# Attention scores as one fp32 product per block instead of three fp32r products, in a kernel of attention, expert layer and FFN

## The chip, the cores and the metric

The kernel runs on one core of a Trainium2 chip. The metric is device time in microseconds (us) of the whole program. A measurement of this kernel is the median of several executions; the profile is one further execution with the hardware profiler on.

## The reference, cut to what matters

Three stages follow each other: block-causal attention (4 batches, 8 heads, 576 rows, head size 64), an expert layer in which each token goes to one of 8 experts, and a dense feed-forward layer (FFN). The change touches only the first stage, and in it only how the scores are made.

```python
# q, k, v: (4, 8, 576, 64)
scores = scale * np.matmul(q, k.transpose(0, 1, 3, 2))      # scale = 1/8
mask = block_i >= block_j                                   # blocks of 64 rows
scores = np.where(mask, scores, -1000000000.0)
scores = scores - np.max(scores, axis=-1, keepdims=True)
attn = np.exp(scores)
attn = attn / (np.sum(attn, axis=-1, keepdims=True) + 1e-09)
attn_out = np.matmul(attn, v)
x = _moe_ref(attn_out as (2304, 512), w_gate, w1, w2)       # argmax expert, two products
return _moe2_ref(x, w_in, w_out)                            # softplus FFN
```

## The kernel before

**Order of the work.** Every engine runs its instructions in the order in which the program issues them, and that order is written out by hand: `SCHEDULE` is a list of step names, and the program calls the steps one after the other. A step belongs to one or two engines, and waits are placed where a tile is written and read. So the order on each engine is the order of its steps in the list.

**Attention.** Two heads of a batch make a pair; there are 16 pairs, and the steps of a pair carry its number (`S1.10` is a step of pair 10). The first head lies in partitions 0 to 63 and the second in 64 to 127 of the transposed operands, so the score products of the two heads (`j` = 0 and 1) use the upper and the lower half of the rows of TensorE's array. The 576 query rows are cut into five chunks: chunk 0 of 64 rows and chunks 1 to 4 of 128 rows; the masks leave 64, 192, 320, 448 and 576 key columns (`NK`) for them. The steps of a pair, in about their order:

- `Kta`, `Qta` (`prep_pe`, L317): four TensorE transposes each of a pair's k and q rows 0 to 511 into a PSUM tile `psT`. `Ktb`, `Qtb`: one transpose each of the last 64 rows.
- `Kha`, `Qha`, `Khb`, `Qhb` (`prep_hi`, L336): ScalarE (ACT) writes the rounded high part of the transposed operand as fp32r, q times 1/8. `Kla`, `Qla`, `Klb`, `Qlb` (`prep_lo`, L342): VectorE (DVE) subtracts that from the original and writes the low part. `kZ` and `qZ` hold both parts.
- `S0`, `S1`, `S2` (`scores`, L348): the score products. `S0` makes chunk 4 of head 0 (576 columns, as two products of 288) and chunks 3 and 0 of head 1 (448 and 64 columns); `S1` makes chunks 3 and 0 of head 0 and chunk 4 of head 1; `S2` makes chunks 2 and 1 of both (320 and 192 columns). Each product is made three times: high by high, low by high, high by low. A short bf16 product of 64 columns adds the mask to the last block of each chunk but chunk 0.
- `m` (`s_max`): the row maximum on DVE, for one chunk and head. `e` (`s_exp`): exponential and row sum on ACT. `T` (`t_pe`): TensorE transposes of the exponentials, 30 a pair, into `pt`. `h` (`t_out`): copies of `pt` into `PT`, banks 0 and 1 on ACT, banks 2 and 3 on DVE.
- `V` (`pv`): twelve fp32 products of `PT` with v; the two heads use the left and the right 64 columns of the array. `F`, `Xa`, `Xb` (`x_pe`): five fp32 products of 144 columns that transpose the result back and make gate logits; `xa`, `xb` (`x_out`): DVE reads them out of PSUM and divides by the row sums.

A pair's products and maxima run one pair ahead of its `T` and `V`, and its transposes of q and k one pair ahead of that. So between `S0` of a pair and the next pair's `S0` TensorE does, in this order: `T`s with the next pair's `Kta` and `Qta` between them, `Xa` and `Xb`, more `T`s, `Ktb` and `Qtb`, `S1`, `S2`, seven `T`s, `V`.

**PSUM.** The pool `pss` has three tiles for `psT` and for the score tiles `s`; `ps1` has two for `pt`; `ps2` has one, which chunk 4's scores (`s4`) and the five products of `x_pe` (`psx`) take in turn; `pso` has one for `V`.

**Loads.** The raw tiles of k, q and v have five column groups; the fifth holds the last 64 rows, which is half a tile, and is loaded twice, into both halves of the partitions.

In the later pairs steps of the expert routing (`er...`) and the first weight conversions of the expert layer stand between the steps of attention, on DVE, ACT and TensorE.

Of the kernel before, what the change touches and what calls it, by code (L numbers as in the profile page):

```python
# [46 lines left out]
f4 f5 at f6 f7 p0 f0 f1 p1 f2 p2 f3 p3 p4 p5 f8 f9 f10 f11 f12 f13 p6 f14 f15 p7 f16 f17 f18 p8 f19 f20 f21 p9 f22 f23  # L47
f24 f25 p10 f26 f27 f28 p11 f29 f30 p12 f31 f32 f33 p13 f34 p14 f35 f36 p15 f37 p16 f38 f39 p17 f40 f41 f42 p18 f43
b1.0 b1.1 p19 b1.2 b1.3 p20 b1.4 b1.5 p21 b1.6 b1.7 b1.8 p22 u0 Kta.0 b1.9 b1.10 b1.11 p23 b1.12 b1.13 p24 b1.14 b1.15
b1.16 p25 b1.17 Kha.0 p26 p27 p28 Qta.0 p29 Kla.0 p30 Ktb.0 p31 Qtb.0 p32 Qha.0 p33 p34 Qhb.0 p35 Khb.0 Qla.0 p36 Qlb.0  # L50
Klb.0 u1 S0.0 m40.0 Kta.1 Qta.1 m31.0 Kha.1 Qha.1 m01.0 et Kla.1 e31.0 Qla.1 Ktb.1 Qtb.1 e40.0 S1.0 Qhb.1 e01.0 Qlb.1
# [5 lines left out]
Ktb.3 Qtb.3 h01.1 h21.1 S1.2 b2.0 La.0 b2.1 b2.2 b2.3 Qhb.3 b2.4 b2.5 Khb.3 b2.6 b2.7 Qlb.3 b2.8 b2.9 Klb.3 b2.10 b2.11
m30.2 S2.2 m41.2 e30.2 m20.2 T11.1 e41.2 m00.2 T30.1 m10.2 e00.2 m21.2 h11.1 m11.2 e20.2 h30.1 V.1 e10.2 e21.2 e11.2
Xr.2 F1.1 S0.3 F0.1 m40.3 T10.2 T20.2 m31.3 h10.2 Kta.4 e40.3 h20.2 T00.2 Qta.4 m01.3 Kha.4 T31.2 h00.2 Kla.4 Xa.1
Qha.4 h31.2 e31.3 Xb.1 Qla.4 T21.2 e01.3 xa.1 T01.2 xb.1 xo.1 Ktb.4 Qtb.4 h01.2 h21.2 S1.3 La.1 Qhb.4 Khb.4 Qlb.4 Klb.4  # L60
m30.3 S2.3 m41.3 e30.3 m20.3 T11.2 e41.3 m00.3 T30.2 m10.3 e00.3 m21.3 h11.2 m11.3 e20.3 h30.2 V.2 e10.3 e21.3 e11.3
# [5 lines left out]
h21.4 S1.5 La.3 Qhb.6 Khb.6 Qlb.6 Klb.6 m30.5 S2.5 m41.5 e30.5 m20.5 T11.4 e41.5 m00.5 T30.4 m10.5 e00.5 m21.5 h11.4
m11.5 e20.5 h30.4 V.4 e10.5 e21.5 e11.5 Xr.5 F1.4 S0.6 F0.4 m40.6 T10.5 T20.5 m31.6 h10.5 Kta.7 e40.6 h20.5 T00.5 Qta.7
m01.6 Kha.7 T31.5 h00.5 Kla.7 Xa.4 Qha.7 h31.5 e31.6 Xb.4 Qla.7 T21.5 e01.6 xa.4 T01.5 xb.4 xo.4 Ktb.7 Qtb.7 h01.5
h21.5 S1.6 b3.0 La.4 b3.1 b3.2 b3.3 Qhb.7 b3.4 b3.5 Khb.7 b3.6 b3.7 Qlb.7 b3.8 b3.9 Klb.7 b3.10 b3.11 m30.6 S2.6 m41.6  # L70
e30.6 m20.6 T11.5 e41.6 m00.6 T30.5 m10.6 e00.6 m21.6 h11.5 m11.6 e20.6 h30.5 V.5 e10.6 e21.6 e11.6 Xr.6 F1.5 S0.7 F0.5
m40.7 T10.6 T20.6 m31.7 h10.6 Kta.8 e40.7 h20.6 T00.6 Qta.8 m01.7 Kha.8 T31.6 h00.6 Kla.8 Xa.5 Qha.8 h31.6 e31.7 Xb.5
Qla.8 T21.6 e01.7 xa.5 T01.6 xb.5 xo.5 Ktb.8 Qtb.8 h01.6 h21.6 S1.7 La.5 Qhb.8 Khb.8 Qlb.8 Klb.8 m30.7 S2.7 m41.7 e30.7
m20.7 T11.6 e41.7 m00.7 T30.6 m10.7 e00.7 m21.7 h11.6 m11.7 e20.7 h30.6 V.6 e10.7 e21.7 e11.7 Xr.7 F1.6 S0.8 F0.6 m40.8
T10.7 T20.7 m31.8 h10.7 Kta.9 e40.8 h20.7 T00.7 Qta.9 m01.8 Kha.9 T31.7 h00.7 Kla.9 Xa.6 Qha.9 h31.7 e31.8 Xb.6 Qla.9
T21.7 e01.8 xa.6 T01.7 xb.6 xo.6 Ktb.9 Qtb.9 h01.7 h21.7 S1.8 La.6 Qhb.9 Khb.9 Qlb.9 Klb.9 m30.8 S2.8 m41.8 e30.8 m20.8
T11.7 e41.8 m00.8 T30.7 m10.8 e00.8 m21.8 h11.7 m11.8 e20.8 h30.7 V.7 e10.8 e21.8 e11.8 Xr.8 F1.7 S0.9 b3.12 F0.7 b3.13
b3.14 b3.15 b3.16 b3.17 m40.9 T10.8 T20.8 m31.9 h10.8 Kta.10 e40.9 h20.8 T00.8 Qta.10 m01.9 Kha.10 T31.8 h00.8 Kla.10
Xa.7 Qha.10 h31.8 e31.9 Xb.7 Qla.10 T21.8 e01.9 xa.7 T01.8 xb.7 xo.7 Ktb.10 Qtb.10 h01.8 h21.8 S1.9 La.7 Qhb.10 Khb.10
Qlb.10 Klb.10 m30.9 S2.9 m41.9 e30.9 m20.9 T11.8 e41.9 m00.9 T30.8 m10.9 e00.9 m21.9 h11.8 m11.9 e20.9 er0 h30.8 V.8  # L80
e10.9 er1 er2 e21.9 er3 er4 e11.9 er5 er6 er39 Xr.9 F1.8 S0.10 F0.8 m40.10 T10.9 T20.9 m31.10 h10.9 Kta.11 e40.10 h20.9
T00.9 Qta.11 m01.10 Kha.11 T31.9 h00.9 Kla.11 Xa.8 Qha.11 h31.9 e31.10 Xb.8 Qla.11 T21.9 e01.10 xa.8 T01.9 xb.8 xo.8
Ktb.11 Qtb.11 h01.9 h21.9 S1.10 La.8 Qhb.11 Khb.11 Qlb.11 Klb.11 m30.10 S2.10 m41.10 e30.10 m20.10 T11.9 e41.10 m00.10
T30.9 m10.10 e00.10 m21.10 er7 h11.9 er8 m11.10 e20.10 er9 er40 er10 er41 e10.10 er11 er42 er12 h30.9 V.9 e21.10 er13
er14 e11.10 er15 er16 er17 Xr.10 er18 er19 er20 er21 er60 wl0 er22 er23 er24 F1.9 wl4 S0.11 F0.9 wl5 m40.11 T10.10 wl6
T20.10 m31.11 h10.10 Kta.12 e40.11 h20.10 wl3 T00.10 Qta.12 m01.11 Kha.12 T31.10 wl7 h00.10 Kla.12 Xa.9 Qha.12 h31.10
e31.11 Xb.9 Qla.12 T21.10 e01.11 xa.9 T01.10 xb.9 xo.9 Ktb.12 Qtb.12 h01.10 h21.10 S1.11 La.9 Qhb.12 Khb.12 Qlb.12
Klb.12 m30.11 S2.11 m41.11 e30.11 m20.11 T11.10 e41.11 m00.11 T30.10 m10.11 e00.11 m21.11 er25 h11.10 er26 m11.11
e20.11 er27 h30.10 V.10 e10.11 er28 er29 e21.11 er30 er31 er33 er32 e11.11 er34 er44 er35 er67 er36 er68 er37 er38
Xr.11 er43 F1.10 er45 S0.12 er61 er46 er62 er47 F0.10 er48 er49 er50 er51 m40.12 T10.11 T20.11 m31.12 h10.11 Kta.13  # L90
e40.12 h20.11 T00.11 Qta.13 m01.12 Kha.13 er52 er53 T31.11 h00.11 Kla.13 Xa.10 Qha.13 er63 h31.11 e31.12 Xb.10 xa.10
# [1431 lines left out]
```

## Time and profile before

| | |
|---|---|
| median of 3 runs | 924.22 us (923.73, 924.22, 932.33) |
| profiled execution | 922.65 us, of which 920.8 us from the first to the last instruction |
| mean granted TensorE clock | 0.994 |
| TensorE busy (matmul) | 898.9 us, 98% |
| VectorE / ScalarE busy | 665.1 us, 72% / 567.8 us, 62% |
| first and last score product | 7.8 us and 215.6 us after the start |

The busy share of TensorE is that of overlapping intervals with modelled ends: a product's shown duration is longer than the time after which the next one starts. So costs are read from starts: from the start of one group of products to the start of the next. Attention takes somewhat more than the first 229 us of the span, with 16 pairs of nearly the same pattern; the rest is the expert layer and the FFN.

### The profile page before, as it was taken

The page shows a single profiled execution, that of the slowest core. Times are in us where ns is not written, and L with a number is a line of the kernel's source. Part 1 is how long each engine was busy: PE and PEld are TensorE (multiplying, and loading weights), DVE is VectorE, ACT ScalarE, POOL GpSimd, SP SyncE. Part 2 cuts the span into 40 slices and gives each one's busy share as a digit, 9 for nine tenths or more (in the row PEclk, how much of TensorE's full clock was granted, in tenths as well). Part 3 has the DMA queues.
Part 4 walks back from the last instruction along what each step waited for, and adds up shares of the span by engine and source line. Part 5 has one row for each costly group of instructions (what it writes and reads, how often), then busy time and mean ns, then how long its engine had stood idle before and what let it go on. Part 6 is the DMA issues. An engine that isn't in the chain of part 4 may idle for free.

```text
span 920.8 us, 18350 instructions
## 1 busy us (share of the span) xinstructions
PE 898.9 (98%) x6340; PEld 793.8 (86%) x6340; DVE 665.1 (72%) x1476; ACT 567.8 (62%) x1256; POOL 137.5 (15%) x181
## 2 busy tenths in 40 slices
...
GB/s 136 190 173 71 141 84 155 68 51 117 173 52 234 106 303 266 245 224 210 209 42 25 86 236 221 173 177 217 234 294 176 227 302 136 145 120 158 120 79 103
DMA packets 138741, 149.17 MB, mean 162 GB/s; under 512 B 70927, under 2 KB 96015, under 8 KB 138640
## 3 DMA queue, kind: packets, MB, share of 16 engines
...
q10 hardware_dynamic: 1344, 0.33, 0.2%
q14 instruction: 50, 0.41, 0.1%
...
## 4 chain that ended last, share of the span: by engine, by line
PE 57%; DVE 4%; DMA 4%; issue 1%; ACT 1%; SPq 0%; DVEq 0%
PE hps L973 3%; PE hps L974 3%; PE hps L975 3%; PE yps L993 3%; PE yps L995 3%; PE yps L994 3%; PE fh L1138 3%; PE fh L1139 3%; PE fh L1137 3%; PE fX L1138 2%; PE fX L1139 2%; PE fX L1137 2%; PE fY L1138 2%; DMA gq<-gd 2%; PE fY L1139 2%; PE fY L1137 2%
## 5 line engine op out<-in xcount | busy, mean ns | idle before, releaser
L1267 ACT CAST ah<-sum 128x1280 fp32r<-128x1280 f32 (+1 forms) x40 | 46.3, 1157 | 107.5 <-DVE sum L1260 35.7
L973 PE MATMUL hps<-xh,H1h 128*128 128x256 f32 x384 | 109.2, 284 | 1.1 <-DVE hl L983 1.1
L974 PE MATMUL hps<-xl,H1h 128*128 128x256 f32 x384 | 108.9, 284 | 0.3 <-DVE xl L963 0.3
L975 PE MATMUL hps<-xh,H1l 128*128 128x256 f32 x384 | 108.8, 283 | 0.0
L385 ACT ACTIVATE P<-s,negm 128x448 f32<-128x448 f32 (+4 forms) x160 | 82.7, 527 | 25.4 <-DVE negm L380 25.4
L936 DVE TENSOR_TENSOR H2l<-R,H2h 128x512 fp32r<-128x512 f32 x96 | 66.5, 709 | 26.7 <-ACT H2h L932 26.7
L380 DVE TENSOR_REDUCE negm<-s 128x1 f32<-128x576 f32 (+4 forms) x160 | 68.1, 478 | 19.7 <-PE s L374 19.7
L993 PE MATMUL yps<-H2h,hh 128*128 128x512 f32 x192 | 77.4, 403 | 2.1 <-PEq L1463 2.1
L932 ACT CAST H2h<-R 128x512 fp32r<-128x512 f32 x96 | 57.9, 620 | 32.4 <-DVE H2l L936 17.8
L973 PEld LDWEIGHTS hps<-xh,H1h 128*128 128x128 f32 x384 | 73.7, 192 | 1.9 <-DVE hl L983 1.3
L995 PE MATMUL yps<-H2l,hh 128*128 128x512 f32 x192 | 75.0, 391 | 0.0
L994 PE MATMUL yps<-H2h,hl 128*128 128x512 f32 x192 | 74.8, 390 | 0.0
L974 PEld LDWEIGHTS hps<-xl,H1h 128*128 128x128 f32 x384 | 73.7, 192 | 0.9 <-DVE xl L963 0.5
L936 DVE TENSOR_TENSOR H1l<-R,H1h 128x512 fp32r<-128x512 f32 x96 | 64.8, 713 | 13.1 <-ACT H1h L932 12.1
L975 PEld LDWEIGHTS hps<-xh,H1l 128*128 128x128 f32 x384 | 73.7, 192 | 0.0
L391 PE MATMUL pt<-ident,P 128*128 128x128 f32 x480 | 69.4, 282 | 2.7 <-DVE PT L396 2.0
...
L932 ACT CAST H1h<-R 128x512 fp32r<-128x512 f32 x96 | 55.1, 619 | 18.7 <-PE hps L974 17.3
L374 PE MATMUL s<-kZ,qZ 64*128 64x288 f32 (+4 forms) x576 | 62.7, 330 | 2.3 <-DVE kZ L345 1.3
L1271 DVE TENSOR_TENSOR al<-sum,ah 128x1280 fp32r<-128x1280 f32 (+1 forms) x40 | 54.3, 1356 | 14.3 <-ACT ah L1267 14.3
L374 PEld LDWEIGHTS s<-kZ,qZ 64*128 64x128 f32 x576 | 52.9, 195 | 10.4 <-issue 6.3
L391 PEld LDWEIGHTS pt<-ident,P 128*128 128x128 f32 x480 | 53.8, 143 | 6.4 <-DVE PT L396 2.7
(330 smaller groups left out, 2616.5 us busy)
## 6 DMA issues: line engine op xcount, KB each, us to landing
...
```

The lines of the kernel that those rows point to most:

```text
L374: mm(o, lhsT=a, rhs=b, start=first, stop=last)
L380: nc.vector.tensor_reduce(m[0:n], SC[p, j, c][0:n], axis=AX.X, op=ALU.max, negate=True)
L385: nc.scalar.activation(t[0:n, 0:NK[c]], SC.pop((p, j, c))[0:n], AF.Exp, bias=NM.pop((p, j, c))[0:n], scale=1.0, accum_out=rs[p % 4][0:n, c ...
L391: nc.tensor.transpose(ps[:, o:o + 128], P[p, j, c][:, 128 * kc:128 * kc + 128], ident)
L932: nc.scalar.copy(HW[l, i][0], raw(l, i))
L936: TT(l_, raw(l, i), h.bitcast(F32), op=ALU.subtract)
L973: mm(a, lhsT=wh, rhs=xh, start=(k == 0), stop=False)
L974: mm(a, lhsT=wh, rhs=xl, start=False, stop=False)
L975: mm(a, lhsT=wl, rhs=xh, start=False, stop=(k == 3))
L993: mm(o, lhsT=h[:, c], rhs=wh, start=(f == 0), stop=False)
L994: mm(o, lhsT=l[:, c], rhs=wh, start=False, stop=False)
L995: mm(o, lhsT=h[:, c], rhs=wl, start=False, stop=(f == 7))
```

## The change

The scores of a block are one product of unsplit fp32 operands instead of three fp32r products. What follows from it in the code:

- `Z` holds one fp32 copy of each transposed operand. k is copied by ACT (`nc.scalar.copy`), q is multiplied by 1/8 by DVE (`tensor_scalar`), and the low-part steps `Kla`, `Qla`, `Klb`, `Qlb` are gone, as is ACT's work for q.
- The last 64 rows of q are loaded into the lower half of k's fifth column group, and one transpose makes both (`Ktb`; `Qtb` is gone). Of the 44 first loads 38 are left, and 16 instead of 18 for each later batch.
- Chunk 0's product uses its own 64 query rows as weights (64 array columns) and not 128 any more.
- The products of the two heads are issued so that the columns sent to each stay level (`sent`), and no longer by index.
- In `SCHEDULE` the removed steps are taken out, `Qha` and `Qhb` stand at about the places of the old `Qla` and `Qlb`, and some first loads, memsets and later loads move by a few places. All steps after attention keep their order.

```diff
 def prep_pe(p, nm, part):
         b, hp = divmod(p, H // 2)
+        ps = PS[p, nm if part == "a" else "4"] = pss.tile([128, 512], F32, tag="s", name="psT")
+        for i, c in enumerate(range(4) if part == "a" else [4]):
+            t = raw[b, nm][:, c, 2 * hp:2 * hp + 2, :].rearrange("p h d -> p (h d)")
+            nc.tensor.transpose(ps[:, 128 * i:128 * i + 128], t, ident)
+
+    def prep_out(p, nm, part):
         if part == "a":
...
+            Z[p, nm] = work.tile([128, S], F32, tag=nm + "Z", name=nm + "Z", bufs=2)
+            src, o = PS.pop((p, nm)), Z[p, nm][:, 0:512]
         else:
...
-        nc.scalar.activation(Z[p, nm][:, 0, sl], src, AF.Copy, scale=0.125 if nm == "q" else 1.0)
-
-    def prep_lo(p, nm, part):
-        src, sl = prep_src(p, nm, part)
-        z = Z[p, nm]
-        nc.vector.scalar_tensor_tensor(z[:, 1, sl], src, 0.125 if nm == "q" else 1.0, z[:, 0, sl].bitcast(F32), op0=ALU.mult, op1=ALU.subtract)
+            x = {"k": 0, "q": 64}[nm]
+            src, o = PS[p, "4"][:, x:x + 64], Z[p, nm][:, 512:576]
+        if nm == "k":
+            nc.scalar.copy(o, src)
+        else:
+            nc.vector.tensor_scalar(o, src, 0.125, None, op0=ALU.mult)
...
             for c, off in what:
-                o, w = SPAN[c][0], NK[c]
+                (o, n), w = SPAN[c], NK[c]
                 out = SC[p, j, c] = s[:, off:off + w]
                 for a, m in ([(0, w)] if w <= 512 else [(0, 288), (288, 288)]):
-                    end = a + m == w
-                    for x, y in ((0, 0), (1, 0), (0, 1)):
-                        last = (x, y) == (0, 1) and not (c and end)
-                        l.append((out[:, a:a + m], q_[x][:, o:o + 128], k_[y][:, a:a + m], (x, y) == (0, 0), last))
+                    l.append((out[0:n, a:a + m], q_[:, o:o + n], k_[:, a:a + m], True, not c or a + m < w))
                 if c:
                     l.append((out[:, w - 64:w], mrow[64 * j:64 * j + 64], mcol[64 * j:64 * j + 64], False, True))
             lists.append(l)
-        for i in range(max(map(len, lists))):
-            for l in lists:
-                if i < len(l):
-                    o, a, b, first, last = l[i]
-                    mm(o, lhsT=a, rhs=b, start=first, stop=last)
+        sent = [0, 0]
+        while any(lists):
+            j = min((i for i in range(2) if lists[i]), key=lambda i: sent[i])
+            o, a, b, first, last = lists[j].pop(0)
+            sent[j] += o.shape[1]
+            mm(o, lhsT=a, rhs=b, start=first, stop=last)
```

Of the schedule, these lines show the pattern of the first pairs:

```diff
-T20.0 m31.1 h10.0 Kta.2 e40.1 h20.0 T00.0 Qta.2 m01.1 Kha.2 Xr.0 T31.0 h00.0 Kla.2 Qha.2 T21.0 h31.0 e31.1 Ktb.2 Qla.2
+e21.0 m40.1 T10.0 e11.0 T20.0 m31.1 h10.0 Kta.2 e40.1 h20.0 T00.0 Qta.2 m01.1 Kha.2 Xr.0 T31.0 h00.0 T21.0 h31.0 e31.1
```

On TensorE, at `S0` of a middle pair, the program before has this order. `s_1197` is the tile of chunk 4 of head 0, the other `s` that of chunks 3 and 0 of head 1, `mcol,mrow` is the mask; the last row is the first `T`. A product of 128 output rows uses 128 columns of the array.

```order
L374 MATMUL s_1197<-kZ,qZ 128x288
L374 LDWEIGHTS mrow
L374 MATMUL s<-mcol,mrow 128x64
L374 MATMUL s_1197<-kZ,qZ 128x288
L374 MATMUL s<-kZ,qZ 128x64
L374 MATMUL s_1197<-kZ,qZ 128x288
L374 MATMUL s<-kZ,qZ 128x64
L374 LDWEIGHTS mrow
L374 MATMUL s_1197<-mcol,mrow 128x64
L374 MATMUL s<-kZ,qZ 128x64
L391 MATMUL pt<-ident,P_0_124 128x128 [waits PE_49]
```

The changed program has this order at the same place (its `scores` is at L357, its `T` at L374).

```order
L357 MATMUL s_1206<-kZ,qZ 128x288 [waits PE_49]
L357 MATMUL s<-kZ,qZ 128x448 [waits PE_49,Activation_49]
L357 MATMUL s_1206<-kZ,qZ 128x288
L357 LDWEIGHTS mrow
L357 MATMUL s<-mcol,mrow 128x64
L357 MATMUL s<-kZ,qZ 64x64
L357 LDWEIGHTS mrow
L357 MATMUL s_1206<-mcol,mrow 128x64
L374 MATMUL pt<-ident,P_2_134 128x128 [waits PE_49]
```

Six products and three short ones of chunk 0 have become two and one, and chunk 0's product, of 64 output rows now, stands between two mask products of 128 output rows.

On DVE, between the row maxima of `S0` and those of `S1`, the program before has this order (`kZ`, `qZ` at L345 are the low parts, `PT` at L396 the copies `h`, `xs` and `lg` the steps `xa` and `xb`).

```order
L380 TENSOR_REDUCE negm<-s 64x1
L345 SCALAR_TENSOR_TENSOR kZ<-psT,kZ 128x512 [waits Activation_49]
L396 COPY PT_1463<-pt 128x320 [waits PE_49]
L345 SCALAR_TENSOR_TENSOR qZ<-psT,qZ 128x512 [waits Activation_49]
L439 TENSOR_TENSOR xs<-psx,rinv 128x384 [waits DMAHW7_49,DMAHW6_49,PE_49]
L440 TENSOR_TENSOR lg<-psx,rinv 128x48 [waits Pool_49]
L439 TENSOR_TENSOR xs<-psx,rinv 128x256
L440 TENSOR_TENSOR lg<-psx,rinv 128x32
L396 COPY PT_1492<-pt 128x512 [waits PE_49]
L345 SCALAR_TENSOR_TENSOR qZ<-psT_1487,qZ 128x64 [waits PE_49,Activation_49]
L345 SCALAR_TENSOR_TENSOR kZ<-psT_1487,kZ 128x64
```

The changed program has this.

```order
L363 TENSOR_REDUCE negm<-s 64x1
L379 COPY PT_1435<-pt 128x320 [waits PE_49]
L330 TENSOR_SCALAR qZ<-psT 128x512
L422 TENSOR_TENSOR xs<-psx,rinv 128x384 [waits DMAHW7_49,DMAHW6_49,PE_49]
L423 TENSOR_TENSOR lg<-psx,rinv 128x48 [waits Pool_49]
L422 TENSOR_TENSOR xs<-psx,rinv 128x256
L423 TENSOR_TENSOR lg<-psx,rinv 128x32
L379 COPY PT_1464<-pt 128x512 [waits PE_49]
L330 TENSOR_SCALAR qZ<-psT 128x64 [waits Activation_49]
```

The two low-part steps of k are gone from this stretch, and q's copies stand where its low-part steps stood.

## Rows read from the trace of the kernel before

**Rows 1.** The page's first part: busy time, share, instructions of each engine.

```profile
PE 898.9 (98%) x6340; PEld 793.8 (86%) x6340; DVE 665.1 (72%) x1476; ACT 567.8 (62%) x1256; POOL 137.5 (15%) x181
```

**Rows 2.** Busy us of each engine in stretches of 25 us, granted clock, DMA share, GB/s.

```profile
100.00:125.00 25.00, 25.00 (x226) 20.66 (x224) 18.03 (x50) 18.20 (x58) 1.07 (x4) 1.00 0.42 80
150.00:175.00 25.00, 23.03 (x213) 19.29 (x209) 23.48 (x89) 15.66 (x48) 1.08 (x4) 1.00 0.45 150
```

**Rows 3.** TensorE's timeline, most of one pair: start us, us, line, operation, count.

```profile
102.00 1.39 PE L421 MATMUL psx<-xrhs,xT 128*128 128x144 f32 x10
103.23 1.04 PE L391 MATMUL pt<-ident,P 128*128 128x128 f32 x8
104.10 0.27 PE L328 MATMUL psT<-ident,kraw 128*128 128x128 f32 x1
104.42 1.12 PE L374 MATMUL s<-kZ,qZ 64*128 64x448 f32 x7
...
105.68 0.69 PE L374 MATMUL s<-kZ,qZ 64*128 64x320 f32 x6
106.20 0.21 PE L374 MATMUL s<-mcol,mrow 64*128 64x64 bf16 x2
...
106.65 0.21 PE L374 MATMUL s<-mcol,mrow 64*128 64x64 bf16 x2
106.79 0.98 PE L391 MATMUL pt<-ident,P 128*128 128x128 f32 x7
107.70 3.68 PE L406 MATMUL o<-PT,vraw 128*64 128x512 f32 x24
111.31 0.92 PE L374 MATMUL s<-kZ,qZ 64*128 64x288 f32 x8
...
112.50 0.33 PE L391 MATMUL pt<-ident,P 128*128 128x128 f32 x1
```

**Rows 4.** The same timeline a few pairs later, around a step `V`.

```profile
203.32 3.35 PE L406 MATMUL o<-PT,vraw 128*64 128x512 f32 x24
206.60 0.69 PE L374 MATMUL s<-kZ,qZ 64*128 64x288 f32 x5
```

**Rows 5.** Timeline of TensorE's weight loads at the start of `S1` of that pair.

```profile
104.41 0.18 PEld L374 LDWEIGHTS s<-kZ,qZ 64*128 64x128 f32 x1 [0.17 <-issue]
104.75 0.42 PEld L374 LDWEIGHTS s<-kZ,qZ 64*128 64x128 f32 x5 [0.16 <-issue]
```

**Rows 6.** Timeline of DVE there; in brackets idle time before, and what ended it.

```profile
101.94 0.69 DVE L345 SCALAR_TENSOR_TENSOR kZ<-psT,kZ 128x512 fp32r<-128x512 f32 x1 [0.57 <-ACT kZ L340]
102.55 0.48 DVE L396 COPY PT<-pt 128x320 f32<-128x320 f32 x1
102.95 0.68 DVE L345 SCALAR_TENSOR_TENSOR qZ<-psT,qZ 128x512 fp32r<-128x512 f32 x1
103.55 0.55 DVE L439 TENSOR_TENSOR xs<-psx,rinv 128x384 f32<-128x384 f32 x1
...
104.45 0.18 DVE L440 TENSOR_TENSOR lg<-psx,rinv 128x32 f32<-128x32 f32 x1
...
105.88 1.29 DVE L380 TENSOR_REDUCE negm<-s 128x1 f32<-128x448 f32 x2 [0.35 <-PE s L374]
```

**Rows 7.** Timeline of ACT: first exponential after `S1`, and the copy `V` waits for.

```profile
106.59 0.63 ACT L385 ACTIVATE P<-s,negm 128x448 f32<-128x448 f32 x1 [1.46 <-DVE negm L380]
...
108.28 0.57 ACT L396 COPY PT<-pt 128x512 f32<-128x512 f32 x1
```

**Rows 8.** TensorE's waits in the first 230 us: total us, times, longest.

```profile
PE s L374 <- DVE kZ L345: 1.3, 2, 1.0
PE psT L328 <- DVE kZ L345: 1.1, 1, 1.1
```

**Rows 9.** Engines in stretches near the start (columns as in Rows 2).

```profile
10.10:13.50 3.40, 1.92 (x13) 1.30 (x13) 2.61 (x10) 3.04 (x10) 0.00 (x0) 1.00 0.50 108
13.50:17.00 3.50, 3.18 (x28) 2.88 (x25) 2.16 (x6) 1.59 (x5) 0.00 (x0) 0.50 0.47 98
```

More of the change, by code (lines that the diff above doesn't have):

```diff
@@ L46 @@
 SCHEDULE = """
[L47 to L51, printed above, removed]
@@ L57 @@
[L57 to L61, printed above, removed]
@@ L67 @@
[L67 to L91, printed above, removed]
@@ new lines @@
+b3.6 b3.7 Qhb.7 b3.8 b3.9 m30.6 S2.6 m41.6 e30.6 m20.6 T11.5 e41.6 m00.6 T30.5 m10.6 e00.6 m21.6 h11.5 m11.6 e20.6
+h30.5 V.5 e10.6 e21.6 e11.6 Xr.6 F1.5 S0.7 F0.5 m40.7 T10.6 T20.6 m31.7 h10.6 Kta.8 e40.7 h20.6 T00.6 Qta.8 m01.7 Kha.8
+T31.6 h00.6 Xa.5 h31.6 e31.7 Xb.5 Qha.8 T21.6 e01.7 xa.5 T01.6 xb.5 xo.5 Ktb.8 h01.6 h21.6 S1.7 La.5 Khb.8 Qhb.8 m30.7
+S2.7 m41.7 e30.7 m20.7 T11.6 e41.7 m00.7 T30.6 m10.7 e00.7 m21.7 h11.6 m11.7 e20.7 h30.6 V.6 e10.7 e21.7 e11.7 Xr.7
+F1.6 S0.8 F0.6 m40.8 T10.7 T20.7 m31.8 h10.7 Kta.9 e40.8 h20.7 T00.7 Qta.9 m01.8 Kha.9 T31.7 h00.7 Xa.6 h31.7 e31.8
```

249 lines of the change are left out of this document (129 added, 120 removed).

## Prediction

> **What bounds the kernel now.** I read the page's busy line first, then stretches of 25 us, then TensorE's timeline of one pair, and then whoever TensorE waits for inside that pair. TensorE is busy for 98% of the span [rows 1] and for all of a middle stretch of attention, where DVE and ACT have some 30% to spare [rows 2]. One pair of heads repeats every 13.15 us with the same rows to 0.1 us. So a pair is priced by TensorE's own starts, and a gain on DVE or ACT counts only where TensorE waits for them.
>
> Inside a pair I found two such waits. In `S1` the second half's first weights start 0.34 us after the first half's [rows 5]: they need the one `ps2` tile, which DVE empties until 104.45 + 0.18 = 104.63 [rows 6]. And `V` takes 3.61 us (107.70 to 111.31) [rows 3] but 3.28 where nothing holds it [rows 4]: its fourth product needs ACT's copy that ends at 108.28 + 0.57 = 108.85 [rows 7], so 0.33 us go there.
>
> **What a score product costs.** The granted clock is 1.00 in these stretches [rows 2], that is 2.4 GHz. The code's five fp32 products of `x_pe` show as ten records in 1.23 us, 0.123 us each [rows 3]; 144 columns would take 0.060 us at one column per clock. So an fp32 product is two passes of two clocks per column: four clocks per column in all. For fp32r, three products of 320 columns per head go from 105.68 to 106.20 [rows 3]: 0.52 us, of which 960 columns at one clock are 0.40 and 0.12 is the first weights and small gaps. Per column the three products cost 3 clocks and the one costs 4. The 192-column blocks do not follow that: 106.20 to 106.65 is 0.45 us for a mask and 576 columns (0.24 us), because each product there waits for its 128 weight columns, about 0.11 us apart. Fewer and longer products lose that.
>
> No row shows fp32 products in the two row halves. The nearest is `V`, fp32 in two column halves: 1856 columns per head at four clocks are 3.09 us, one head after the other would be 6.2, and 3.28 is seen [rows 4]. So the halves overlap, and both passes of a product in one half do not hold up the other half. I take the same for row halves; the other end is in the rivals.
>
> **Part by part, per pair.**
>
> `S2`: the 320 block is 1280 clocks, 0.53 + 0.12 = 0.65 us against 0.52; the 192 block 768 clocks, 0.32, plus about 0.10 for weights, against 0.41: nothing. `S2` gains 0.12 us of length.
>
> `S0`: head 0's chain is four passes of 288 columns, 4 x 0.24 + 0.12 = 1.08 us, against six of 0.12 to 0.13 plus 0.12 now, 0.89. Before, the tail after it was the third 64-column product of head 1, and the whole was 1.19 (111.31 to 112.50) [rows 3]. With mask (0.03) and the change to full-size transposes (0.10, next paragraph) the new length would be 1.21: +0.02 only.
>
> **The tile shape.** Chunk 0 now uses 64 rows by 64 columns of the array, between products of 64 by 128. Where the shape changes today TensorE stands still: two transposes of 0.109 us from 104.10 end at 104.32 and `S1` starts at 104.42; the last masks from 106.65 end at 106.69 and the transposes start at 106.79; seven transposes, with 0.05 for first weights, end at 107.60 and `V` starts at 107.70 [rows 3]. That is 0.10 us for each of three kinds of change, and the third alters the columns alone, as chunk 0 does. So I take 0.10 per change, two more in `S0` and two in `S1`, and that a change waits for both halves to run empty. The bounds are 0 (a half may change by itself, or the shape within a half may not matter) and this. `S0` then is 1.08 + 0.10 + weights and two passes of 64 columns (0.16) + 0.10 + mask (0.05) + 0.10 = 1.59: +0.40 us.
>
> The Trainium skill, in TensorEngine Tiling (Key Properties), says that changing the tiling mode, and not just the tile, drains TensorE, and lists 64x128 and 64x64 as different modes. The 0.10 us gaps agree for the changes that this trace has; no row here shows the change between those two.
>
> `S1`: one transpose less (`Qtb`) lets it start 0.11 us earlier, at 104.31. DVE no longer runs k's low part (0.69) ahead of the `PT` copy, whose transposes end at 102.00 plus some 0.2 of latency; so copy, q's scaling and `xs` come 0.35 us earlier [rows 6]. The scaling is a form not in the trace; 0.48 to 0.68 by the two `PT` copies, and I take 0.68, the row of its own size. `ps2` is free at 104.28, head 1's chain starts at 104.40 and is through 1.08 later, 105.48. Shape change, chunk 0, change back and mask: 0.41, so `S2` starts at 105.89, not 105.68. `S2` is 1.23 long where it is 1.11: the seven `T`s start at 107.12 against 106.79: +0.33 us (without the shape cost 106.74: -0.05).
>
> `V`: the copy it waits for hangs on the first row maximum after `S1`, at 105.88 [rows 6], 1.46 after `S1`'s start, then on ACT [rows 7]. The tile it reads is complete when chunk 0's product is through, 105.74 + 0.2 = 105.95: 0.1 later than now, while `V` starts 0.33 later. So 0.22 of the wait of 0.33 go. Without the shape cost the maximum comes 0.36 earlier and the whole wait goes, 0.31.
>
> Sum for a pair: 0.40 + 0.33 - 0.22 = +0.51; 16 pairs +8.2 us. Without the shape cost: 0.02 - 0.05 - 0.31 = -0.34; -5.4 us.
>
> **Once only.** In two routing pairs `S2` waits 1.3 us for k's low part [rows 8], which the schedule had behind routing steps on DVE; it is gone, and `Qhb` stands ahead of those steps: -1.7 us with what follows (0 to -3, since other DVE work is queued there too). At the start a transpose waits 1.1 us for the first low part [rows 8]; now the tile is free when ACT has copied k, but `Qha` on DVE comes behind three row maxima, so I take -0.6 (0 to -1.5). Loads are fewer by 6 and 2 per batch; TensorE is full while they run, so nothing. ACT loses about 0.9 us a pair and DVE as much; only what is counted above reaches TensorE. Everything after attention keeps its order and starts that much later.
>
> The granted clock falls to 0.50 from 13.5 us, after a stretch in which TensorE was busy 1.92 of 3.40 us [rows 9]. If `S1` of pair 0 comes early enough to keep it at 1.00, some 3 us of the slow 10 come back (the exponentials of pair 0 bound part of it). I take it that it falls again.
>
> **The sum.** 922.65 + 8.2 - 1.7 - 0.6 = 928.6 against the profiled execution, which lay 1 to 1.6 us under the two close timed runs: 929.5 us for the median, 0.6% over 924.22.
>
> **Rivals.**
>
> A: chunk 0's shape costs nothing, or empties only its own half. For it: no row shows that change, and mask products of another type pass without a gap. Against it: all three kinds of change in the trace cost 0.10, one of them in columns alone. 922.65 - 5.4 - 2.3 + 1 = 916 us.
>
> B: products of the two halves start strictly in program order. Both passes of a product stand together in the program, so a half's second pass would hold the other half's first; with the levelled order `S2` then runs its two blocks in four steps and not three: +0.35 us, `S0` +0.13, `S1` +0.25, together 0.73 a pair, 11.7 us on top: 941 us. It decides once the halves do not slide past each other by more than one pass. Against it: `V` has its passes in the same order and takes 3.28 us; in program order it would be 3.09 + 0.43 for the first product's extra step + 0.15 = 3.7.
>
> The Trainium skill, in TensorE: Matmul & The Clock Gate (The mechanism), states that order: matmuls start and end in program order. The 3.28 us of `V` speak against it for column halves; nothing here shows row halves of fp32.
>
> C: the clock stays up at the start: 926.5 us, on top of the forecast.
>
> **How the numbers follow.** Forecast 50%, A 28%, B 10%, C 12%. The forecast's own range is 925 to 934 (0 to 3 us of routing wait, the bounds of the start, 0.05 to 0.11 of `V`'s wait a pair). The range of 8 in 10 reaches down to A's far side and stops short of B: 914 to 936. About 1% is what a measurement of this kernel can tell from no change, that is 915 to 933.4. Faster: 0.4 of A, 0.11. Slower: B and a quarter of the forecast, 0.22. The rest, 0.67, is the same.
>
> **What would show it.** In the changed profile: score records at two clocks a column (288 columns 0.24 us apart); gaps of 0.10 us on both sides of each 64x64 product, and `S0` 1.59 us long (A: 1.21; B: over 1.7 with `S2` at 1.6); the second half of `S1` starting within 0.1 us of the first; `V` at 3.4; a pair at 13.65. A row half that waits for the other outside chunk 0, or DVE late with q's scaling, would make the prediction wrong.

## The result and the profile after

The changed kernel took 932.88 us (median of 20 runs, 929.59 to 938.74), the kernel before on the same chip 924.72 us (20 runs, 921.68 to 932.33). The ratio is 1.009 with a 95% interval of 1.0071 to 1.0108: slower by 0.9%, clear of the noise but inside the 1% that the prediction took for no change, and 3.4 us over the forecast. The profiled execution took 931.68 us, 929.9 of them from the first to the last instruction; before it was 920.8.

The page's busy line and one stretch of 25 us (columns as in [rows 1, 2]):

```profile
PE 905.8 (97%) x6132; PEld 785.3 (84%) x6132; DVE 653.4 (70%) x1444; ACT 557.9 (60%) x1224; POOL 151.1 (16%) x181
100.00:125.00 25.00, 25.00 (x189) 19.50 (x191) 16.75 (x43) 15.77 (x50) 1.07 (x4) 1.00 0.36 66
```

DVE and ACT lose some 10 us each, TensorE gains 7. TensorE still fills this middle stretch, so that the pair has to be read from starts again. TensorE's timeline of one pair of the changed kernel, from `S0` (columns as in [rows 3]):

```profile
98.74 1.24 PE L357 MATMUL s<-kZ,qZ 64*128 64x288 f32 x6
99.60 0.19 PE L357 MATMUL s<-mcol,mrow 64*128 64x64 bf16 x1
99.91 0.32 PE L357 MATMUL s<-kZ,qZ 64*64 64x64 f32 x2
100.16 0.20 PE L357 MATMUL s<-mcol,mrow 64*128 64x64 bf16 x1
100.29 0.33 PE L374 MATMUL pt<-ident,P 128*128 128x128 f32 x1
...
102.94 1.39 PE L404 MATMUL psx<-xrhs,xT 128*128 128x144 f32 x10
104.17 1.04 PE L374 MATMUL pt<-ident,P 128*128 128x128 f32 x8
105.04 0.27 PE L318 MATMUL psT<-ident,kraw 128*128 128x128 f32 x1
105.24 1.09 PE L357 MATMUL s<-kZ,qZ 64*128 64x448 f32 x4
...
107.00 0.82 PE L357 MATMUL s<-kZ,qZ 64*128 64x320 f32 x4
107.65 0.21 PE L357 MATMUL s<-mcol,mrow 64*128 64x64 bf16 x2
107.68 0.58 PE L357 MATMUL s<-kZ,qZ 64*128 64x192 f32 x4
108.08 0.21 PE L357 MATMUL s<-mcol,mrow 64*128 64x64 bf16 x2
108.22 0.99 PE L374 MATMUL pt<-ident,P 128*128 128x128 f32 x7
109.14 3.48 PE L389 MATMUL o<-PT,vraw 128*64 128x512 f32 x24
112.55 0.65 PE L357 MATMUL s<-kZ,qZ 64*128 64x288 f32 x2
```

A pair now takes 112.55 - 98.74 = 13.81 us, 13.80 as the mean of the first eight, where it took 13.15. `S0` is 100.29 - 98.74 = 1.55 (1.19 before), the stretch from the last-rows transpose to the seven `T`s 108.22 - 105.04 = 3.18 (2.69), `V` 3.41 (3.61): +0.36, +0.49 and -0.20, together +0.65.

What holds `S1`'s second half stands in three views. TensorE's weight loads show when each half begins; the second row is the second half's first load:

```profile
105.24 0.64 PEld L357 LDWEIGHTS s<-kZ,qZ 64*128 64x128 f32 x4 [0.17 <-issue]
105.58 0.18 PEld L357 LDWEIGHTS s<-kZ,qZ 64*128 64x128 f32 x1
```

DVE before it, and ACT behind it (columns as in [rows 6, 7]):

```profile
103.14 0.49 DVE L379 COPY PT<-pt 128x320 f32<-128x320 f32 x1 [0.73 <-PE pt L374]
103.55 0.68 DVE L330 TENSOR_SCALAR qZ<-psT 128x512 f32<-128x512 f32 x1
104.37 0.56 DVE L422 TENSOR_TENSOR xs<-psx,rinv 128x384 f32<-128x384 f32 x1
...
105.29 0.18 DVE L423 TENSOR_TENSOR lg<-psx,rinv 128x32 f32<-128x32 f32 x1
...
109.51 0.57 ACT L379 COPY PT<-pt 128x512 f32<-128x512 f32 x1
```

The second half starts 105.58 - 105.24 = 0.34 us after the first, as before the change [rows 5], 0.11 after DVE's `lg` has emptied the `ps2` tile (105.29 + 0.18 = 105.47). DVE lost the two low-part steps of k and now stands idle for 0.73 us ahead of the `PT` copy, but `xs` starts hardly sooner in relation to TensorE: 1.43 us after `psx` begins (102.94 to 104.37), where it was 1.55 (102.00 to 103.55) [rows 3, 6].

The start went otherwise than in the profile before. Windows of three profiles, where [rows 9] have a granted clock of 0.50 for the same stretch: the changed kernel, the same kernel profiled once more, and the changed kernel with one ACT step moved (`e4_h11` below; the step stands behind this stretch):

```profile
13.50:17.00 3.50, 2.47 (x21) 1.67 (x20) 2.74 (x7) 2.67 (x11) 0.00 (x0) 1.00 0.73 165
```

```profile
13.50:17.00 3.50, 2.48 (x21) 1.54 (x17) 2.53 (x7) 3.06 (x12) 0.00 (x0) 1.00 0.73 165
```

```profile
13.50:17.00 3.50, 3.50 (x17) 2.19 (x17) 1.73 (x4) 1.50 (x4) 0.00 (x0) 0.50 0.71 161
```

Attention, to the first transpose of the expert layer, ends 4.9 us later than before in the first profile and 4.4 in the second. That transpose before, and in the two profiles of the changed kernel:

```profile
229.51 0.33 PE L955 MATMUL t<-ident,xg 128*128 128x128 f32 x1
```

```profile
234.42 0.33 PE L938 MATMUL t<-ident,xg 128*128 128x128 f32 x1
```

```profile
233.91 0.33 PE L938 MATMUL t<-ident,xg 128*128 128x128 f32 x1
```

From there to the end it took 691.3 us before, 929.9 - 234.4 = 695.5 in the first profile after and 926.8 - 233.9 = 692.9 in the second. In the first the granted clock falls once before the last 3 us, behind a stretch (780 to 784 us) in which TensorE was busy for 1.59 of 4.00 us; in the second it is 1.00 there:

```profile
784.20:787.50 3.30, 3.30 (x15) 3.12 (x16) 3.30 (x9) 0.39 (x2) 0.00 (x0) 0.50 0.53 155
```

### The profile page after: what moved, and what is told of

Its sections match the earlier page's. It is cut to its first block, busy times and chain, and to the rows that moved or that the text cites. A ratio compares the mean times of both kernels' runs of the same rounds, so it can differ in the third digit from the quotient of the medians.

```text
span 929.9 us, 17823 instructions
## 1 busy us (share of the span) xinstructions
PE 905.8 (97%) x6132; PEld 785.3 (84%) x6132; DVE 653.4 (70%) x1444; ACT 557.9 (60%) x1224; POOL 151.1 (16%) x181
## 4 chain that ended last, share of the span: by engine, by line
PE 57%; DVE 3%; DMA 3%; SPq 1%; issue 1%; ACT 1%; DVEq 0%
PE yps L976 4%; PE yps L977 4%; PE yps L978 4%; PE hps L956 3%; PE hps L957 3%; PE hps L958 3%; PE fh L1121 3%; PE fh L1122 3%; PE fh L1120 3%; DMA gq<-gd 2%; PE fX L1121 2%; PE fX L1122 2%; PE fX L1120 2%; PE fY L1121 2%; PE fY L1120 2%; PE fY L1122 2%
## 5 line engine op out<-in xcount | busy, mean ns | idle before, releaser
L368 ACT ACTIVATE P<-s,negm 128x448 f32<-128x448 f32 (+4 forms) x160 | 82.7, 527 | 29.5 <-DVE negm L363 29.1
L1315 POOL DMA_INDIRECT out_dram<-fos,OI x16 | 46.9, 2932 | 202.1 <-DVE fos L1307 163.3
L357 PE MATMUL s<-kZ,qZ 64*128 64x288 f32 (+4 forms) x384 | 72.2, 420 | 2.4 <-DVE qZ L330 1.4
L374 PE MATMUL pt<-ident,P 128*128 128x128 f32 x480 | 68.1, 279 | 2.1 <-DVE PT L379 1.3
L357 PEld LDWEIGHTS s<-kZ,qZ 64*128 64x128 f32 (+1 forms) x384 | 42.1, 177 | 25.5 <-issue 17.5
L379 ACT COPY PT<-pt 128x512 f32<-128x512 f32 x64 | 37.5, 586 | 39.6 <-PE pt L374 39.5
```

The costliest lines, as they stand in the source:

```text
L357: mm(o, lhsT=a, rhs=b, start=first, stop=last)
L368: nc.scalar.activation(t[0:n, 0:NK[c]], SC.pop((p, j, c))[0:n], AF.Exp, bias=NM.pop((p, j, c))[0:n], scale=1.0, accum_out=rs[p % 4][0:n, c ...
L374: nc.tensor.transpose(ps[:, o:o + 128], P[p, j, c][:, 128 * kc:128 * kc + 128], ident)
```

## The experiments

All ratios are against the kernel before on the same chip (924.2 to 924.8 us). Differences from the changed kernel are from its 932.88 us; in two later runs (`after_again`) it took 928.71, so they are uncertain by some 4 us, and what the traces show stands beside them. The theory after the result: chunk 0's 64-column fp32 product has the array emptied on both sides (D), and `S1` and `V` wait for DVE and ACT (W, V).

**`e1_wide0`: chunk 0 on 128 columns again.**

```diff
-l.append((out[0:n, a:a + m], q_[:, o:o + n], k_[:, a:a + m], True, not c or a + m < w))
+l.append((out[:, a:a + m], q_[:, o:o + 128], k_[:, a:a + m], True, not c or a + m < w))
```

> The changed kernel with chunk 0's product on 128 query columns again, so that no product of the scores has another tile shape than its neighbours. Theory D (a change between 64x128 and 64x64 empties both halves of the array and costs 0.09 us on each side): S0 falls from 1.55 to 1.21 us, S1 by about 0.31, V loses its remaining wait of 0.13; a pair takes 13.0 us and the kernel about 920 us, 12 under the changed kernel and 3 to 5 under the one before. Rival N (the length comes from the fp32 columns and from waits, the shape does not matter): S0 stays at 1.5 and the kernel within 2 us of the changed one's 932.

Measured: 923.86 us, ratio 0.9991 (0.9971 to 1.0011), 9.0 us under the changed kernel (4.9 under its two later runs). TensorE's timeline of `S0`:

```profile
95.54 1.23 PE L357 MATMUL s<-kZ,qZ 64*128 64x288 f32 x6
96.40 0.19 PE L357 MATMUL s<-mcol,mrow 64*128 64x64 bf16 x1
96.43 0.41 PE L357 MATMUL s<-kZ,qZ 64*128 64x64 f32 x2
96.61 0.19 PE L357 MATMUL s<-mcol,mrow 64*128 64x64 bf16 x1
96.77 0.44 PE L374 MATMUL pt<-ident,P 128*128 128x128 f32 x2
```

Between the first mask and chunk 0 there are 0.03 us instead of 99.91 - 99.60 = 0.31 above, and `S0` takes 1.23 instead of 1.55. The pair falls to 13.26, not to the 13.0 expected, since `V` did not lose its wait but rose from 3.41 to 3.54 us. In the two profiles attention ends 7.5 us sooner (226.91 against 234.42). So the shape of that one product is what makes the change slower: all the rest of it, fp32 scores included, neither costs nor gains anything that can be measured.

**`e2_narrow0`: 64 columns for chunk 0 in the kernel before, with its three fp32r products.**

```diff
...
-l.append((out[:, a:a + m], q_[x][:, o:o + 128], k_[y][:, a:a + m], (x, y) == (0, 0), last))
+l.append((out[0:n, a:a + m], q_[x][:, o:o + n], k_[y][:, a:a + m], (x, y) == (0, 0), last))
```

> The kernel before with chunk 0's three products on 64 columns: the shape of the change alone. Their places, between products of the other head, are unchanged. Theory D: up to five changes of shape in each S0 and S1 at 0.09 us and with the other half empty; S0 goes from 1.19 to about 2 us, S1 as much, and the kernel to 945 to 955 us. Rival N: within 2 us of the kernel before.

Measured: 921.66 us, ratio 0.9971 (0.9951 to 0.999). `S0` on TensorE:

```profile
99.78 0.93 PE L374 MATMUL s<-kZ,qZ 64*128 64x288 f32 x8
100.50 0.20 PE L374 MATMUL s<-mcol,mrow 64*128 64x64 bf16 x1
100.53 0.34 PE L374 MATMUL s<-kZ,qZ 64*64 64x64 f32 x4
100.69 0.20 PE L374 MATMUL s<-mcol,mrow 64*128 64x64 bf16 x1
100.82 0.44 PE L391 MATMUL pt<-ident,P 128*128 128x128 f32 x2
```

The narrow products follow the mask after 0.03 us and `S0` is shorter than before, 1.04 us against 1.19. D as I had it, that a change between 64 by 128 and 64 by 64 empties the array whatever the type, fell here.

**`e10_c0f`: one fp32 product of 64 by 64 among the fp32r products.** It leaves out chunk 0's low parts.

```diff
+if not c:
+    l.append((out[0:64, a:a + m], q_[0][:, o:o + 64].bitcast(F32), k_[0][:, a:a + m].bitcast(F32), True, True))
+    continue
 for x, y in ((0, 0), (1, 0), (0, 1)):
```

> The kernel before, in which chunk 0 is one fp32 product of 64 query columns of the high parts (q and k rounded) among fp32r products of 128; its two low-part products are left out, all else is as before. Theory F (an fp32 product of 64 by 64 has the array empty on both sides, whatever stands beside it; fp32r of the same shape does not): a gap of 0.09 us on each side of the chunk-0 product in S0 and S1, S0 about 1.30 us (1.04 with narrow fp32r products, 1.19 before), S1+S2 about 2.5, pair 13.2 to 13.4, total 924 to 928. Rival G (the gap in the changed kernel comes from the neighbours being fp32, or from the order of the mask products): no gap, S0 1.04 or less, pair 13.0, total 921.

Measured: 927.84 us, ratio 1.0042 (1.0027 to 1.0057). `S0`, 100.50 to 101.98, TensorE's timeline and, under it, its weight loads:

```profile
100.50 0.92 PE L377 MATMUL s<-kZ,qZ 64*128 64x288 f32 x8
101.23 0.20 PE L377 MATMUL s<-mcol,mrow 64*128 64x64 bf16 x1
101.36 0.65 PE L377 MATMUL s<-kZ,qZ 64*64 64x64 f32 x3
101.86 0.20 PE L377 MATMUL s<-mcol,mrow 64*128 64x64 bf16 x1
```

```profile
101.22 0.09 PEld L377 LDWEIGHTS <-mrow 64*128 64x128 bf16 x1
101.36 0.44 PEld L377 LDWEIGHTS s<-kZ,qZ 64*64 64x64 f32 x3
```

The mask is through 0.03 us after 101.23, and the next weights start at 101.36: the gap of 0.10 us is back, though all neighbours are fp32r. (The third record of that group is head 0's last product, which the row counts with the other two; it starts at 101.61, about 0.10 us after the narrow product is through.) `S0` is 1.48 us long, above the 1.30 expected, and a pair 13.57, above the 13.2 to 13.4: two products less in `S0` and yet 0.45 us more than `e2_narrow0`. No gap stands before an fp32 product of 128 columns (`e1_wide0`) or an fp32r product of 64 (`e2_narrow0`). So it is the fp32 product of this shape that empties the array, not the shape alone and not its neighbours. The Trainium skill, in TensorEngine Tiling (Key Properties), names a drain for every change of tiling mode; `e10_c0f` agrees for fp32 and `e2_narrow0` (0.03 us) does not for fp32r, and the measurement decides.

**`e4_h11` and `e6_before_h11`: the copy that `V` waits for, one place earlier on ACT**, in 13 pairs of the changed kernel and of the kernel before.

```diff
-m10.5 e00.5 m21.5 h11.4
+m10.5 h11.4 e00.5 m21.5
```

> The changed kernel with ACT's copy h11 one place earlier, ahead of the exponential e00. If V's fourth product waits for that copy, V falls from 3.41 to 3.28 us and the kernel by about 2 us. If V's length has another cause (fp32 in the two halves), V stays at 3.41 and the time too.

> The kernel before with h11 (ACT's copy that V waits for) put ahead of the next pair's e00 on ACT in 13 pairs. Theory V (the whole wait of 0.33 us in V is that copy): V 3.61 to 3.28-3.35 us, pair 13.15 to 12.85, total 924.2 to 920. Rival (T11 itself or the tile of its bank comes late, so the copy cannot start sooner): V 3.5 or more, total 923 to 924.

Measured: 929.37 us, ratio 1.0049 (1.0025 to 1.0074), and 920.90 us, ratio 0.9962 (0.9947 to 0.9977). In the changed kernel `V` goes from 3.41 to 3.28 us and the total falls by 3.5, of which 13 times 0.13 explains 1.7; in the kernel before `V` goes from 3.61 to 3.33 and the total falls by 3.9 (13 times 0.28 is 3.6). That copy was the whole wait in the first and 0.28 of the 0.33 us in the second. TensorE's row of `V` in the second:

```profile
106.72 3.40 PE L407 MATMUL o<-PT,vraw 128*64 128x512 f32 x24
110.05 0.92 PE L375 MATMUL s<-kZ,qZ 64*128 64x288 f32 x8
```

**`e3_merged`: the shared last rows alone**, in the kernel before (one tile, one transpose, the loads as in the changed kernel).

```diff
...
-if nm == "k":
-    PS[p, "4"] = pss.tile([128, 512], F32, tag="s", name="psT4")
-ps, cs, off = PS[p, "4"], [4], {"k": 0, "q": 128}[nm] - 512
+if nm == "q":
+    return
+PS[p, "4"] = pss.tile([128, 512], F32, tag="s", name="psT4")
+ps, cs, off = PS[p, "4"], [4], -512
...
```

> The kernel before with k's and q's last rows in one tile and one transpose (loads and transposes of the change, scores and splits as before). If TensorE's own time counts, one transpose of 0.109 us less per pair: 1.7 us faster. Theory W (the second half of S1 starts when DVE has emptied the tile of x_pe, which starts only after the last of its ten records): the transpose ends earlier and S1's second half starts when it did, so the wait grows by 0.1 and the kernel stays within 1 us.

Measured: 921.31 us, ratio 0.9961 (0.9939 to 0.9983). In the pair the transpose's 0.11 us are gained and lost again: 0.20 + 2.49 = 2.69 us to the `T`s, exactly as before (0.31 + 2.38), since `S1`'s second half starts when it did. The profiled execution is no shorter either (920.8 us, as before), but its granted clock is 0.50 from 341.6 to 344.9 us, where the profile before has 1.00. The median's 2.9 us are more than either theory had; where they come from I did not find.

**`e11_xearly`: `x_pe` ahead of `T31`**, `xs` on DVE behind the copy `h31`.

```diff
-T31.4 h00.4 Xa.3 h31.4 e31.5 Xb.3 Qha.6 T21.4 e01.5 xa.3 T01.4 xb.3
+Xa.3 Xb.3 T31.4 h00.4 h31.4 xa.3 xb.3 e31.5 Qha.6 T21.4 e01.5 T01.4
```

> The changed kernel with Xa and Xb (x_pe) put ahead of T31 in 14 pairs, and xa and xb on DVE behind h31, so that DVE empties the one ps2 tile earlier. Theory W (S1's second half starts 0.34 us late since xs on DVE can begin only after the last of psx's ten records): the 0.34 us go, S1+S2 2.98 to 2.64 us, V's wait stays at 0.13 to 0.3, pair 13.80 to 13.45 to 13.6, total 926 to 929 against 932.9. Rival (the second half starts late for its weights or for the order in which the two halves take turns): S1+S2 stays at 2.98, total 932.

Measured: 935.58 us, ratio 1.0136 (1.011 to 1.0161): slower, and `S1` and `S2` together at 2.95. That looks like the rival, but the edit did not do what it was for. DVE's timeline:

```profile
105.91 0.49 DVE L380 COPY PT<-pt 128x320 f32<-128x320 f32 x1 [1.96 <-PE pt L375]
106.32 0.55 DVE L423 TENSOR_TENSOR xs<-psx,rinv 128x384 f32<-128x384 f32 x1
```

`h31` needs `T31`, which now stood behind `x_pe`; DVE idled 1.96 us for it, and `xs`, behind `h31`, came even later after `psx` began (104.15 to 106.32, 2.17 us). The four `T`s behind waited too. It tells nothing between the theories, so I made the next one.

**`e14_qlate`: q's four transposes behind `Xb`, q's scaling behind `h21`**, so that `psx` can come up to 0.44 us sooner and nothing on DVE stands between `h31` and `xs`.

```diff
-T00.4 Qta.6 m01.5 Kha.6 T31.4 h00.4 Xa.3 h31.4 e31.5 Xb.3 Qha.6 T21.4 e01.5 xa.3 T01.4 xb.3 xo.3 Ktb.6 h01.4 h21.4 S1.5 La.3 Khb.6 Qhb.6
+T00.4 m01.5 Kha.6 T31.4 h00.4 Xa.3 h31.4 e31.5 Xb.3 Qta.6 T21.4 e01.5 xa.3 T01.4 xb.3 xo.3 Ktb.6 h01.4 h21.4 S1.5 La.3 Khb.6 Qha.6 Qhb.6
```

> The changed kernel with q's four transposes (Qta) put behind Xb, and q's scaling (Qha) on DVE put behind the copy h21, in 13 pairs. So the ten records of psx start 0.44 us earlier, and xs is DVE's next work after h31. Theory W (S1's second half waits for the ps2 tile, which DVE's xs and lg empty, and these can begin only after psx's last record): lg ends about 0.4 us earlier, the 0.34 us at the start of S1 go, S1+S2 2.98 to about 2.64, V's wait stays at 0.13 to 0.3, pair 13.80 to 13.45 to 13.6, total 926 to 929 against 932.9. Rival (the second half starts late for its weights or for the order in which the halves take turns): S1+S2 stays at 2.95 to 2.98, total 932 or more.

Measured: 929.20 us, ratio 1.0063 (1.004 to 1.0086), 3.7 us under the changed kernel's 932.88, but no less than its two later runs on this same chip (928.71). From `V` of pair 0 to `V` of pair 15 the trace has 0.9 us less (203.85 against 204.73). `S1` and `S2` together take 2.64 us, to the hundredth what W said. DVE's timeline, then two rows of TensorE's weight loads:

```profile
105.23 0.49 DVE L380 COPY PT<-pt 128x320 f32<-128x320 f32 x1 [0.52 <-PE pt L375]
106.46 0.56 DVE L423 TENSOR_TENSOR xs<-psx,rinv 128x384 f32<-128x384 f32 x1 [0.74 <-PE psx L405]
...
107.38 0.18 DVE L424 TENSOR_TENSOR lg<-psx,rinv 128x32 f32<-128x32 f32 x1
```

```profile
104.64 0.31 PEld L375 LDWEIGHTS pt<-ident,P 128*128 128x128 f32 x3 [0.24 <-DVE PT L380]
...
107.77 0.54 PEld L358 LDWEIGHTS s<-kZ,qZ 64*128 64x128 f32 x5 [0.17 <-issue]
```

DVE stands idle for `psx` itself now (0.74 us), and `xs` starts again 1.43 us after `psx` begins (105.03 to 106.46), as it does in `e1_wide0` (99.41 to 100.84): that is the floor. `lg` ends at 107.56, ahead of `S1` at 107.77, and both halves load weights at once, so that five loads fit in the first 0.54 us where it was four in 0.64. W is shown for this wait; what it is worth in the total is not. A part is given back elsewhere: the `T`s that now come sooner wait 0.24 us for a `PT` tile, so that `psx` begins 0.21 us sooner behind `S0` and not 0.44, and a pair is 13.70 instead of 13.45.

**`e12_fp32r_best`, `e15_wide0_h11_qlate`, `e16_fp32r_best_qlate`: parts put together.** The first is the kernel before (three fp32r products) with the edits of `e2_narrow0`, `e3_merged` and `e6_before_h11`; the second the changed kernel with those of `e1_wide0`, `e4_h11` and `e14_qlate`; the third is the first with `Qta` behind `Xb`, and on DVE q's low part behind `xs` and the copy `h21` behind all low parts:

```diff
-T00.4 Qta.6 m01.5 Kha.6 T31.4 h00.4 Kla.6 Xa.3 Qha.6 h31.4 e31.5 Xb.3 Qla.6 T21.4 e01.5 xa.3 T01.4 xb.3 xo.3 Ktb.6 Qtb.6 h01.4 h21.4 S1.5 La.3 Qhb.6 Khb.6 Qlb.6 Klb.6
+T00.4 m01.5 Kha.6 T31.4 h00.4 Kla.6 Xa.3 h31.4 e31.5 Xb.3 Qta.6 T21.4 Qha.6 e01.5 xa.3 T01.4 xb.3 Qla.6 xo.3 Ktb.6 Qtb.6 h01.4 S1.5 La.3 Qhb.6 Khb.6 Qlb.6 Klb.6 h21.4
```

> The kernel before (three fp32r products) with only these parts: the shared tile and transpose of the last rows, chunk 0 on 64 query columns, and h11 ahead of e00. If the parts add: S0 1.04, S1+S2+psT about 2.8, V 3.28-3.4, pair 12.65 to 12.8; total 924.2 - 2.9 - 2.5 - 4 = 915. Rival: they share a cause, so that less than half adds: 919 to 921.

> The changed kernel with three edits at once: chunk 0 on 128 query columns, h11 ahead of e00, and Qta and Qha later as in the run beside it. If the three add (9.0 + 3.5 + 4): S0 1.23, S1+S2 2.3, V 3.28, pair 12.75, total 916. If the fp32 products themselves set a floor that the edits do not reach (S1+S2 stays at 2.6): pair 13.0, total 920.

> The fp32r kernel with the shared last rows, narrow chunk 0 and h11 ahead (916.1), and also Qta behind Xb, with q's and k's later low parts ahead of h21 on DVE, in 12 pairs. Theory W holds there too: S1+S2 2.49 to 2.15-2.2, pair 12.65 to 12.35, total 911 to 913. Rival (three low parts in a row on DVE hold up S2's tiles or the first maximum): S1+S2 2.4 or more, or V longer by as much, total 915 to 918.

Measured: 916.06 us, ratio 0.9917 (0.9896 to 0.9938); 919.64 us, ratio 0.9954 (0.994 to 0.9968); 920.79 us, ratio 0.9959 (0.9944 to 0.9974). The three small edits of the first add up (2.5 + 2.9 + 3.9 = 9.3 expected from their own runs, 8.7 measured), a pair takes 12.68 us, and it is the best version of all. The second beats the kernel before too, with a pair of 12.97, but its edits add up to less than was hoped (12.75 and 916). The third is slower even than the rival's 915 to 918: three low parts on DVE between `xs` and the first maximum hold up `S2`, whose first weights load at 102.80, 0.12 us after the last low part ends (102.68), and `V` rises to 3.51 us:

```profile
101.22 0.69 DVE L348 SCALAR_TENSOR_TENSOR qZ<-psT,qZ 128x512 fp32r<-128x512 f32 x1
102.33 0.22 DVE L348 SCALAR_TENSOR_TENSOR qZ<-psT,qZ 128x64 fp32r<-128x64 f32 x1 [0.41 <-ACT kZ L343]
...
103.20 2.73 DVE L383 TENSOR_REDUCE negm<-s 128x1 f32<-128x448 f32 x7
```

The maxima begin 1.67 us after `S1` (which starts at 101.53), where they began 1.46 after it before the change [rows 3, 6].

**`after_again`: the changed kernel once more.**

> The changed kernel once more, unaltered, for a second profile of it. If the stretch from the first transposes of the expert layer to the end (691.3 us before, 695.5 in the first profile of the changed kernel) varies from execution to execution, it differs from 695.5 by over 1 us; if the change sets it, it is 695 to 696. The granted clock in the first 30 us, which stayed at 1.00 in the first profile, may fall to 0.50 in this one: then S1 of pair 1 comes some 3 us later.

Measured: 928.71 us in two runs (ratio 1.0053, 1.0034 to 1.0073). The clock stayed up at the start again, and the stretch behind attention took 692.9 us, not 695.5. Over the fourteen profiles of this study that stretch, whose order of work no edit changed, took 690.1 (`e14_qlate`) to 696.9 us (`e1_wide0`), 694.8 in `e6_before_h11`, which keeps the three fp32r products. The two longest are the only ones with a granted clock of 0.50 near 780 us (`e1_wide0` from 777.2 to 784.0, the first profile of the changed kernel from 784.2 to 787.5). So a single profile says nothing of less than some 5 us there, and I put none of it down to the change.

## Why the prediction was right, and where it was not

It foresaw 0.6% slower and the time came out 0.9% slower, inside its range and inside the 1% either side. Of its mechanism, a shape change that eats what the other parts give back, `e1_wide0` shows the first half: without the shape a pair is 0.54 us shorter. But the shape was to cost 0.85 (+0.51 with it, -0.34 without), and the other parts give nothing back: without the shape a pair takes 13.26, 0.11 more than before the change. Both were taken too large, and in the sum they cancel in part; so do, in the profiled execution, the clock that stayed up (-2.7 us) and the stretch behind attention (+4.2), neither of which was in the sum. That the total came so close is in part luck. By its steps:

- **Four clocks per column, halves side by side.** Right. `S2` was put at 1.23 us and is 108.22 - 107.00 = 1.22; its 320 block is 0.65 us to its masks (107.00 to 107.65), as worked out. Rival B (program order of the halves) needed `S2` at 1.6 and `S0` over 1.7, and neither is there.
- **The tile shape, 0.10 us on each side.** Right in size (`S0` 1.55, forecast 1.59) and for this kernel, wrong in its reason: the 0.10 us were taken from changes of any type in the trace, and `e2_narrow0` shows that fp32r makes the same change for 0.03. Only the fp32 product pays. Rival A (nothing) is out, since `S0` falls to 1.23 without the shape (`e1_wide0`), and its 916 us were out of reach too: that run took 923.86.
- **`S1`: +0.33 us with the transpose saved.** This term failed; it is +0.49. I had `ps2` free 0.35 us sooner because DVE lost k's low part, and so a wait of 0.34 at the second half shrinking to 0.09. `xs` had only 0.12 us to win: it cannot start before `psx` is complete, 1.43 us after it begins. The wait stayed at 0.34, the transpose's gain went into it, and `e14_qlate` took it away by starting `psx` sooner. The wait alone would have made the term +0.58; some 0.08 came back, most of it since the first products of `S2` start at 107.00 together with the last mask of `S1` and not behind it. In all that is 0.16 us a pair, 2.6 us over 16. The same wait of 0.34 stands in `e1_wide0` (weights at 101.72 and 102.06); there the stretch is +0.14, where -0.05 was forecast without the shape cost, and `V` 3.54, where it was 3.30. These two are why the other parts give nothing back.
- **`V`: -0.22.** Measured -0.20, and by `e4_h11` the rest of the wait is the same copy.
- **The pair: +0.51 forecast, +0.65 measured**, all of the difference from `S1`.
- **The routing wait, -1.7.** The wait for k's low part [rows 8] is gone. From the `V` of pair 8 to that of pair 15 the changed kernel takes 2.1 us more (94.39 against 92.25). The score products of six pairs lie in between (none between the last two `V`s); at 0.65 they would make 3.9, so 1.8 came back. This term was right.
- **The start.** I took the clock to fall as before, and gave rival C 12%. In both profiles of the changed kernel it stayed at 1.00, and `V` of pair 0 came 2.4 us sooner than before (26.4 against 28.8); in `e4_h11` and `e14_qlate`, whose order of work is the same up to there, it fell to 0.50 and that `V` came at 29.1. So my price of 3 us was about right. My reading that it hangs on how early `S1` of pair 0 comes is not borne out: the clock fell after an `S1` at 11.9 us (`e4_h11`, `e14_qlate`), but in `e6_before_h11`, which has the order of the kernel before up to there, it was 1.00 from 13.5 to 17.0 us with `S1` at 12.4. It differs from execution to execution, with the old order too. TensorE was busy for the same 2.22 of the 3.50 us from 10 us on in the first profile of the changed kernel and in `e4_h11`, so those rows do not tell what decides. Of the 20 timed runs of the changed kernel, 8 have a mean clock of 0.987 to 0.991 and took 933.1 to 938.7 us; 12 have 0.993 to 0.999 and took 929.6 to 935.5. That mean does not say where the clock fell: the kernel before has 0.994 with a fall at the start alone, the first profile after 0.997 with one at 784 us and one in the last 3.
- **Behind attention** I had nothing. The 4.2 us of the first profile there were 1.6 in the second, and the fourteen profiles differ by more. What it adds to the median of 20 runs stays open.

The sum by its measured terms, for a clock that falls: 922.65 + 0.3 up to the first `V` (29.1 against 28.8; the scores of two pairs are in it) + 14 x 0.65 for the other pairs - 1.8 = 930.3 us for the profiled execution, and with the clock up 2.7 less. What the forecast's 928.6 lacked is in the main the 0.16 a pair of `S1`; of the rest of the way to the median, the start and the stretch behind attention can make it up, and no run separates them.
